# Block 0's first four SwiGLU tiles with tokens as output rows, turned back by four transposing DMAs

## The chip, the cores and the metric

The kernel runs on one core of a Trainium2 chip. The metric is the device time of one launch in microseconds (us), median of several runs of the same program. A profiled execution of the same program gives the page and the trace: which engine did what and when.

## The reference

One layer with two branches over the same layer-normalised input, for 2048 tokens of width 512:

```python
x  = A_x                                   # [1, 2048, 512]
xn = _layernorm(x, axis=-1)
# branch A: diagonal state space, 512 complex states
dt      = exp(log_dt);  Lam_bar = exp(dt * Lam)
Bu      = einsum("bld,pd->blp", xn, ((Lam_bar - 1) / Lam)[:, None] * Bmat)
h_t     = Lam_bar * h_{t-1} + Bu_t         # over the 2048 tokens
yA      = 2 * einsum("blp,dp->bld", h, Cmat).real + xn * Dskip
# branch B: SwiGLU, F = 1792
yB      = (silu(xn @ w1) * (xn @ w3)) @ w2
return x + yA + yB
```

Inputs and output are bf16.

## The kernel before

The 2048 tokens are cut into 4 blocks of 512 (`TBLK`), a block into 4 chunks of 128 tokens (`CPB`). For each block b the kernel makes these things:

- **The normalised block.** `xn_blk[b]` holds it with tokens on the partitions, `xnT_blk[b]` turned, with the width on the partitions (4 parts `dt` of 128). Block 0 is turned by TensorE in four pieces, one for each chunk (`ln_first_transpose`, L236), copied out of PSUM by ScalarE (L244). Blocks 1 to 3 are turned by transposing DMAs on SP (`ln_transpose`, L246).
- **The gates** (`glu`, L581; the last block in `glu_last`, L838). F is 14 tiles of 128 (`NFT`). For a tile f, TensorE (PE) makes gate and up, each 4 matmuls with a 128x128 piece of w1 or w3 as the stationary operand and 512 tokens of xnT streaming (L587). So the output has F on the partitions and tokens along the row. ScalarE (ACT) takes both out of PSUM as bf16, one with Silu, one as a copy (`evac`, L596 and L597), into a pair of tiles `g16`, `u16` for two f. VectorE (DVE) multiplies such a pair (`gate`, L604) into `act(b)`, a tile of 22 columns k of 128 for each chunk: 14 gates and 8 state parts. `act` has two buffers, `g16` and `u16` three each, gate and up four PSUM banks (`ps_gu`).
- **The states.** `bu` (L444), or `bu_fast` (L760) for blocks 2 and 3, makes the inputs u of the recurrence. `bu_fast` uses a product scheme with 7 instead of 8 products: sums of quarters are multiplied, and two quarters of u are a product in PSUM plus a shared product `s5` (`add`, L792, on DVE). `ssm_tasks` (L462) turns u by the angle tables `tabe` (`pre_a`, `pre_b`, `pre_c`), scans it (L505) and turns it back into `act(b)` (`post_a` to `post_c`); some of the sums there are accumulating DMAs issued from GpSimd's queue (POOL).
- **The output** (`y_fast`, L1036): gates and states of two chunks against w2 and the turned C, also with 7 products (L1054), with sums of rows by DVE (`row_sums`, L992: L1000) or by accumulating DMAs ahead of it. DVE's adds (L1065, L1139) and ACT's copies (L1077) read the products out of PSUM.

PE's order is written out by hand. DVE's order is that of a small planner, `Filler`: background tasks with costs are put out when the planned DVE time is not more than a lead past the planned PE time. Matmul groups move PE's clock (`bg.tensor(1.72)` for a tile f), and work that must stand at its place moves DVE's (`bg.own`). ACT's spare steps stand in a list of their own, `sins`: the Sin tables (L384) and other steps, of which one is taken for each f.

**The start of block 0** is special. w1 and w3 come in pieces: tiles 0 and 1 first, then 2 and 3, then the rest (`load_w`, L155). The first `FIRST` = 3 tiles are made in quarters, one for each chunk of tokens, as the chunks come ready. They have six PSUM banks (`first_ps`: four of `ps_gu`, two of `ps_bu`):

```python
637            quarter(0, (0, 1), 2)
638            quarter(1, (0, 1))
639            pps = params_transpose()
...
643            ln_first_transpose(2)
644            quarter(0, (2,))
645            ln_first_transpose(3)
646            quarter(1, (2,))
...
649            quarter(2, range(FIRST))
650            for f in range(FIRST):
651                quarter(3, (f,))
```

From f = 3 on the usual loop runs, and at f = 8 (`MID`) it puts block 0's `bu` in.

**SP's queue** at that time holds, in order: the loads of `bulk_loads`, the four transposes of block 1, then `late_loads` (L182: w2, dskip, x of blocks 2 and 3).

Of the kernel before, what the change touches and what calls it, by code (L numbers as in the profile page):

```python
# [11 lines left out]
ALU = mybir.AluOpType  # L12
# [5 lines left out]
P = 128  # L18
# [45 lines left out]
def kernel(  # L64
# [29 lines left out]
    FIRST = 3  # L94
# [87 lines left out]
    def late_loads():  # L182
        nc.sync.dma_start(out=w2_sb, in_=B_w2.rearrange("(t p) d -> p t d", p=P))
        nc.sync.dma_start(out=dskip_row, in_=A_Dskip.partition_broadcast(P))
        load_x(2, 4)
        load_x(3)

# [3 lines left out]
                for i in range(2 * FIRST)]  # L191
# [235 lines left out]

    def act_gates(b, f):
        k0, k1 = k_gate(f), k_gate(f + 1)
        return act(b)[:, :, k0:k1 + 1:k1 - k0, :].rearrange("p c k t -> p k c t")  # L430
# [31 lines left out]
    def ssm_tasks(b, posts_last=False, between=(), middle=(), late=()):  # L462
# [5 lines left out]
        def half(hf):  # L468
# [3 lines left out]
            def pre_a():  # L472
                if b == 0:
                    sin_step((2 * hf + 1, 1))
                    nc.vector.tensor_scalar(out=tabe[:, psl, 2, :], in0=tabe[:, psl, 1, :], scalar1=-1.0,
                                            scalar2=None, op0=ALU.mult)
                st["g"] = u_blk[b, hf]
                if (b, hf) == (3, 0):
                    st["p"] = up.tile(FULL, BF16, name="u")
                elif b == NBLK - 1:  # L480
                    st["p"] = xtp.tile([P, NDT, TBLK], BF16, name="xnT").rearrange("p (j r) t -> p j r t", r=2)
                else:
                    st["p"] = ssmw.tile(FULL, BF16, name="p")
                nc.vector.tensor_tensor(out=st["p"][:, :, ::-1, :], in0=st["g"], in1=tabe[:, psl, 2:0:-1, :],
                                        op=ALU.mult)

            def pre_b():
                nc.vector.tensor_tensor(out=st["g"], in0=st["g"], in1=tabe[:, psl, 0:1, :].to_broadcast(FULL),  # L488
                                        op=ALU.mult)
# [91 lines left out]
    def glu(b):  # L581
# [26 lines left out]
        if b == 0:  # L608
            f0 = FIRST
            tiles = first_ps  # L610

            def quarter(cl, fs, parts=1):
                tsl = slice(cl * P, (cl + 1) * P)
                n = NDT // parts
                for side, w in ((0, w1_sb), (1, w3_sb)):
                    for i in range(0, NDT, n):
                        for f in fs:
                            for dt in range(i, i + n):
                                nc.tensor.matmul(out=tiles[2 * f + side][:, tsl], lhsT=w[:, dt, f * P:(f + 1) * P],  # L619
                                                 rhs=xnT[:, dt, tsl], start=(dt == 0), stop=(dt == NDT - 1))  # L620

            ln_stats(0, 0)
# [14 lines left out]
            quarter(0, (0, 1), 2)  # L637
            quarter(1, (0, 1))
# [17 lines left out]
            bg.tensor(0.0)  # L656
            bg.fill()
        for f in range(f0, NFT):
# [101 lines left out]
    def bu_fast(b, hf):  # L760
# [9 lines left out]
        s5 = glup.tile([P, 2, TBLK], BF16, name="g16").bitcast(FP32).rearrange("p a t -> p (a t)")  # L770
# [19 lines left out]
        def add(out, ps):  # L790
            bg.own(0.7)
            nc.vector.tensor_tensor(out=out, in0=parts(ps), in1=parts(s5), op=ALU.add)  # L792
# [490 lines left out]
```

## Time and profile before

| | |
|---|---|
| time, 3 runs | 201.09 us median (201.04, 201.09, 201.39) |
| profiled execution, span from the first to the last instruction | 199.5 us |
| profiled execution, own time | not listed beside the three runs; their median is 1.59 us above the span |
| granted TensorE clock in the span | 0.999 of full speed |
| busy: PE matmul, DVE, ACT, POOL | 195.6, 181.8, 135.0, 51.5 us |
| DMA | 25.12 MB, mean 126 GB/s |

Busy time is the sum of an engine's instructions. PE's matmuls overlap each other in the pipeline, so their spacing in the chain is a better price for one than its own duration. PEld is TensorE's loading of the stationary operand. In a line of the trace "L619" is line 619 of the kernel, "out<-in" names the tiles, and a part in brackets says how long the engine was idle ahead of it and what ended that. "Landing" of a DMA is the time from its issue to its completion.

### The profile page before, as it was taken

To read this page: it belongs to the slowest core of one execution; us is meant where nothing else is said; L and a number is where in the kernel's file an instruction comes from. 1 tells how busy PE (TensorE), PEld (TensorE's weight loads), DVE (VectorE), ACT (ScalarE), POOL (GpSimd) and SP (SyncE) were. 2 spreads that over 40 slices of the span, in tenths; PEclk is the share of its full clock that TensorE was granted. 3 is DMA by queue.
4 is the path that set the end of the run, shared out by engine and by line. 5 is a ranking of instruction groups with operands and counts; after the bars stand their busy time and mean duration, and the time that the engine had idled before them with its cause. 6 is when DMAs were issued, how large, how long until landed. Compare 5 with 4: busy or idle time off the path is not lost.

```text
span 199.5 us, 3700 instructions
## 1 busy us (share of the span) xinstructions
PE 195.6 (98%) x1401; PEld 130.7 (65%) x1401; DVE 181.8 (91%) x254; ACT 135.0 (68%) x281; POOL 51.5 (26%) x75
## 2 busy tenths in 40 slices
PE   8999999999999999999999999999999999999994
PEld 2774444444444488866555468888566678888893
DVE  3689699999999999989999997999999999999972
ACT  4699897699999996968998684362588783111220
POOL 7180289700411134041202305040021303310000
PEclk9999999999999999999999999999999999999999
DMA  4999996991497054730997455838137732941111
GB/s 138 326 277 200 302 186 124 343 273 23 69 181 141 0 105 82 135 105 0 156 148 119 89 92 98 172 83 132 53 59 129 149 56 52 174 92 36 53 44 40
DMA packets 32258, 25.12 MB, mean 126 GB/s; under 512 B 16240, under 2 KB 29936, under 8 KB 32240
## 3 DMA queue, kind: packets, MB, share of 16 engines
q0 software_dynamic: 6128, 11.38, 33.5%
q1 hardware_dynamic: 25536, 13.21, 26.8%
q10 hardware_dynamic: 576, 0.30, 0.5%
q8 instruction: 11, 0.18, 0.4%
q14 instruction: 7, 0.06, 0.1%
HBM read 7.74 MB, written 2.10 MB: 49 GB/s over the span
## 4 chain that ended last, share of the span: by engine, by line
PE 95%; DMA 2%; SPq 1%; issue 0%; DVE 0%
PE gu_ps L587 34%; PE gu_ps L1054 17%; PE y_ps L1054 10%; PE gu_ps L848 7%; PE bu_ps L1054 7%; PE bu_ps L454 3%; PE y_ps L454 3%; PE y_ps L869 3%; PE y_ps L780 3%; DMA w_sb<-in_B_w_dram 2%; PE gu_ps L619 2%; PE gu_ps L780 2%; PE bu_ps L869 1%; PE bu_ps L780 1%; PE bu_ps L619 1%; SPq L166 0%
## 5 line engine op out<-in xcount | busy, mean ns | idle before, releaser
L587 PE MATMUL gu_ps<-xnT,w_sb 128*128 128x512 bf16 x312 | 69.6, 379 | 0.0
L587 PEld LDWEIGHTS <-w_sb 128*128 128x128 bf16 x312 | 30.5, 98 | 34.2
L1054 PEld LDWEIGHTS <-act 128*128 128x128 f16 x462 | 43.5, 98 | 5.4
L596 ACT ACTIVATE g<-gu_ps 128x512 bf16<-128x512 f32 x41 | 24.8, 606 | 6.0 <-PE gu_ps L587 3.6
L597 ACT ACTIVATE u<-gu_ps 128x512 bf16<-128x512 f32 x41 | 24.8, 606 | 4.5 <-PE gu_ps L587 3.7
L505 DVE TENSOR_TENSOR_SCAN u<-rho,ends,u 128x512 bf16<-128x512 f32 x16 | 20.0, 1270 | 0.0
L527 POOL DMA_DIRECT2D act<-p x7 | 9.2, 1320 | 34.0 <-DVE act L519 22.1
L1054 PE MATMUL gu_ps<-w_sb,act 128*128 128x256 bf16 (+3 forms) x126 | 16.0, 267 | 0.0
L848 PE MATMUL gu_ps<-xnT,w_sb 128*128 128x512 bf16 x64 | 15.9, 379 | 0.0
L604 DVE TENSOR_TENSOR act<-g,u 128x1024 f16<-128x1024 bf16 x21 | 14.2, 679 | 0.4 <-ACT u L597 0.4
L860 ACT ACTIVATE g<-gu_ps 128x512 bf16<-128x512 f32 x14 | 8.4, 599 | 5.4 <-PE gu_ps L848 5.0
L454 PEld LDWEIGHTS <-bt 128*128 128x128 bf16 x64 | 6.3, 98 | 7.5
L1077 ACT ACTIVATE x_blk<-gu_ps 128x256 f32<-128x256 f32 (+1 forms) x9 | 3.3, 368 | 10.6 <-PE gu_ps L1054 10.6
L1054 PE MATMUL bu_ps<-w_sb,act 128*128 128x256 bf16 (+3 forms) x84 | 10.4, 264 | 0.0
L1054 PE MATMUL gu_ps<-ct,act 128*128 128x256 f16 (+1 forms) x72 | 10.4, 267 | 0.0
L848 PEld LDWEIGHTS <-w_sb 128*128 128x128 bf16 x64 | 6.3, 98 | 4.8
L505 DVE TENSOR_TENSOR_SCAN u<-rho,u 128x512 bf16<-128x512 f32 x8 | 9.2, 1206 | 0.0
L1054 PEld LDWEIGHTS <-x_blk 128*128 128x128 f16 x88 | 8.6, 98 | 1.0
L1054 PEld LDWEIGHTS <-tw 128*128 128x128 f16 x88 | 8.6, 98 | 1.0
L513 DVE TENSOR_TENSOR p<-u,tabe 128x2048 f16<-128x2048 bf16 (+1 forms) x8 | 8.7, 1085 | 0.1
L519 DVE TENSOR_TENSOR act<-u,tabe 128x2048 f16<-128x2048 bf16 (+1 forms) x8 | 8.7, 1083 | 0.0
L488 DVE TENSOR_TENSOR u<-u,tabe 128x2048 bf16<-128x2048 bf16 x7 | 8.5, 1219 | 0.1
(203 smaller groups left out, 392.5 us busy)
## 6 DMA issues: line engine op xcount, KB each, us to landing
act<-p POOLq DMA_DIRECT2D x6, 512.0 KB, 6.1
xn<-x_blk POOLq DMA_DIRECT2D x4, 512.0 KB, 5.5
out_dram<-xn SPq DMA_DIRECT2D x15, 128.0 KB, 1.7
w_sb<-in_B_w_dram SPq DMA_DIRECT2D x1, 1792.0 KB, 8.2
act<-act POOLq DMA_DIRECT2D x5, 352.0 KB, 4.6
w_sb<-in_B_w_dram SPq DMA_DIRECT2D x2, 768.0 KB, 6.4
u<-p POOLq DMA_DIRECT2D x3, 512.0 KB, 5.1
w_sb<-in_B_w_dram SPq DMA_DIRECT2D x4, 256.0 KB, 4.9
```

What stands on the lines that cost most here:

```text
L454: nc.tensor.matmul(out=ps, lhsT=bt[:, ri, dt, pt * P:(pt + 1) * P], rhs=xnT_blk[b][:, dt, :], start=(dt == 0), stop=(dt == NDT - 1))
L505: nc.vector.tensor_tensor_scan(out=v, data0=rho[:, pt:pt + 1].to_broadcast([P, TBLK]), data1=v, initial=init, op0=ALU.mult, op1=ALU.add)
L513: nc.vector.tensor_tensor(out=by_state(st["p16"][:, csl]), in0=by_chunk(st["g"][:, :, ::-1, tsl]), in1=by_chunk(tabe[:, psl, 2:0:-1, tsl]) ...
L519: nc.vector.tensor_tensor(out=by_state(act_state(b, hf)[:, csl]), in0=by_chunk(st["g"][:, :, :, tsl]), in1=by_chunk(tabe[:, psl, 0:1, tsl] ...
L527: gp.dma_start(out=a, in_=p16, accum_op=ALU.add)
L587: nc.tensor.matmul(out=ps[:, tsl], lhsT=w[:, dt, f * P:(f + 1) * P], rhs=xnT[:, dt, tsl], start=(dt == 0), stop=(dt == NDT - 1))
L596: nc.scalar.activation(out=g16[:, f % 2, :], in_=g_ps, func=ACT.Silu)
L597: nc.scalar.activation(out=u16[:, f % 2, :], in_=u_ps, func=ACT.Copy)
L604: nc.vector.tensor_tensor(out=act_gates(b, f - 1), in0=split(g16), in1=split(u16), op=ALU.mult)
L780: nc.tensor.matmul(out=out[:, h * TH:(h + 1) * TH], lhsT=left[:, h, k, :], rhs=right[:, k, :], start=(start and h == 0 and k == 0), stop=( ...
L848: nc.tensor.matmul(out=ps, lhsT=w[:, dt, f * P:(f + 1) * P], rhs=xnT[:, dt, :], start=(dt == 0), stop=(dt == NDT - 1))
L1054: nc.tensor.matmul(out=out, lhsT=left[:, k, :], rhs=right[k][:, cols], start=(start and k == 0), stop=(k == NK - 1), skip_group_check=True)
```

## The change

The first four tiles of block 0 (`FIRST` = 4) are made the other way round. The chunk of xnT is the stationary operand and the columns of w1 or w3 stream, so the output has 128 tokens on the partitions and columns of F along the row: for the chunks 0 and 1 in two halves of 256 columns (A and B, as the weights come), for the chunks 2 and 3 in 512 columns at once. Each chunk has a bank for gate and one for up; those of chunk 3 come from `ps_y`. ACT takes out a chunk's gate and up (`evac_rows`), DVE multiplies two chunks at a time (`gate_rows`) into a part of `act(1)` that is not in use yet (`first_products`), and four transposing DMAs at the end of `late_loads` turn the products back into `act(0)`, one for each chunk.

The diff also changes the state inputs of block 3: where DVE added a product in PSUM and `s5`, ACT now copies the product to u in fp16, and an accumulating DMA from POOL's queue adds `s5`, now fp16 too. `pre_a` and `pre_b` read that u as fp16 and write bf16 in its place.

```diff
-    FIRST = 3
+    FIRST = 4
...
         load_x(2, 4)
         load_x(3)
+        for c in range(CPB):
+            nc.sync.dma_start_transpose(out=act(0)[:, c, 0:FIRST, :], in_=first_products()[:, c, :])
...
+    def first_products():
+        return act(1)[:, :, 2 * NK - FIRST:2 * NK, :].rearrange("p c k t -> p c (k t)")
...
-                st["g"] = u_blk[b, hf]
+                st["v"] = u_blk[b, hf]
+                st["g"] = st["v"].bitcast(BF16) if b in (3,) else st["v"]
...
-                nc.vector.tensor_tensor(out=st["p"][:, :, ::-1, :], in0=st["g"], in1=tabe[:, psl, 2:0:-1, :],
+                nc.vector.tensor_tensor(out=st["p"][:, :, ::-1, :], in0=st["v"], in1=tabe[:, psl, 2:0:-1, :],
...
-                nc.vector.tensor_tensor(out=st["g"], in0=st["g"], in1=tabe[:, psl, 0:1, :].to_broadcast(FULL),
+                nc.vector.tensor_tensor(out=st["g"], in0=st["v"], in1=tabe[:, psl, 0:1, :].to_broadcast(FULL),
...
-            tiles = first_ps
-
-            def quarter(cl, fs, parts=1):
-                tsl = slice(cl * P, (cl + 1) * P)
+            act(0)
+            tiles = [first_ps[2 * c:2 * c + 2] for c in range(CPB - 1)]
+
+            def rows(cl, side, fsl, parts=1):
                 n = NDT // parts
-                for side, w in ((0, w1_sb), (1, w3_sb)):
-                    for i in range(0, NDT, n):
-                        for f in fs:
-                            for dt in range(i, i + n):
-                                nc.tensor.matmul(out=tiles[2 * f + side][:, tsl], lhsT=w[:, dt, f * P:(f + 1) * P],
-                                                 rhs=xnT[:, dt, tsl], start=(dt == 0), stop=(dt == NDT - 1))
-
+                w = (w1_sb, w3_sb)[side]
+                for i in range(0, NDT, n):
+                    for dt in range(i, i + n):
+                        nc.tensor.matmul(out=tiles[cl][side][:, fsl], lhsT=xnT[:, dt, cl * P:(cl + 1) * P],
+                                         rhs=w[:, dt, fsl], start=(dt == 0), stop=(dt == NDT - 1))
+
+            def evac_rows(cl):
+                if cl % 2 == 0:
+                    pair[:] = [glup.tile([P, 2, TBLK], BF16, name="g16"), glup.tile([P, 2, TBLK], BF16, name="u16")]
+                nc.scalar.activation(out=pair[0][:, cl % 2, :], in_=tiles[cl][0], func=ACT.Silu)
+                nc.scalar.activation(out=pair[1][:, cl % 2, :], in_=tiles[cl][1], func=ACT.Copy)
+
+            def gate_rows(cl, g16, u16):
+                bg.own(0.6, -0.5)
+                nc.vector.tensor_tensor(out=first_products()[:, cl:cl + 2, :], in0=g16, in1=u16, op=ALU.mult)
+
+            A, B, AB = slice(0, 2 * P), slice(2 * P, 4 * P), slice(0, 4 * P)
...
-            quarter(0, (0, 1), 2)
-            quarter(1, (0, 1))
+            for side in range(2):
+                for cl in range(2):
+                    rows(cl, side, A)
             pps = params_transpose()
...
             ln_first_transpose(2)
-            quarter(0, (2,))
+            for cl in range(2):
+                rows(cl, 0, B)
             ln_first_transpose(3)
-            quarter(1, (2,))
+            for cl in range(2):
+                rows(cl, 1, B)
...
-            quarter(2, range(FIRST))
-            for f in range(FIRST):
-                quarter(3, (f,))
-            evac(0, tiles[0], tiles[1])
-            evac(1, tiles[2], tiles[3])
-            evac(2, tiles[4], tiles[5])
-            gate()
+            for side in range(2):
+                rows(2, side, AB)
+            tiles.append([ps_y.tile([P, TBLK], FP32, name="y_ps") for _ in range(2)])
+            for side in range(2):
+                rows(3, side, AB)
+            evac_rows(0)
+            evac_rows(1)
+            gate_rows(0, *pair)
+            evac_rows(2)
+            evac_rows(3)
+            late = list(pair)
...
+            if b == 0 and f == FIRST:
+                gate_rows(2, *late)
...
-        s5 = glup.tile([P, 2, TBLK], BF16, name="g16").bitcast(FP32).rearrange("p a t -> p (a t)")
+        by_dma = b in (3,)
+        if by_dma:
+            u = u.bitcast(FP16)
+            s5 = glup.tile([P, 2, TBLK], BF16, name="g16").bitcast(FP16)[:, 0, :]
+        else:
+            s5 = glup.tile([P, 2, TBLK], BF16, name="g16").bitcast(FP32).rearrange("p a t -> p (a t)")
...
         def add(out, ps):
+            if by_dma:
+                copy(out, parts(ps))
+                gp.dma_start(out=out, in_=parts(s5), accum_op=ALU.add)
+                return
             bg.own(0.7)
             nc.vector.tensor_tensor(out=out, in0=parts(ps), in1=parts(s5), op=ALU.add)
```

More of the change, by code (lines that the diff above doesn't have):

```diff
@@ L186, in late_loads @@
         load_x(3)
+        for c in range(CPB):
+            nc.sync.dma_start_transpose(out=act(0)[:, c, 0:FIRST, :], in_=first_products()[:, c, :])
     ones = nc.const_aps.tensor(1.0, (P, TBLK), BF16)
     first_ps = [(ps_gu if i < 4 else ps_bu).tile([P, TBLK], FP32, name="gu_ps" if i < 4 else "bu_ps")
-                for i in range(2 * FIRST)]
+                for i in range(6)]
     wps = first_ps[-1]
```

## The prediction

> **What bounds the kernel now.** I read the page first: engine shares, then the chain that ended last.
>
> ```profile
> PE 195.6 (98%) x1401; PEld 130.7 (65%) x1401; DVE 181.8 (91%) x254; ACT 135.0 (68%) x281; POOL 51.5 (26%) x75
> ...
> PE 95%; DMA 2%; SPq 1%; issue 0%; DVE 0%
> ```
>
> TensorE (PE) is the chain for 95% of the span. VectorE (DVE) at 91% is nearly as full, but nothing on the chain waits for it. Next the chain in order of time (start, length, what), which shows where PE work begins to follow PE work:
>
> ```profile
> 2.58 4.53 DMA w_sb<-in_B_w_dram
> 7.11 0.05 issue
> 7.16 1.51 PE gu_ps L619 x24
> 8.67 0.11 PE y_ps L315
> 8.78 0.33 PE y_ps L243 x4
> 9.11 0.58 PE bu_ps L619 x8
> 9.69 0.22 PE y_ps L243 x4
> 9.92 0.45 PE bu_ps L619 x8
> ...
> 13.04 8.63 PE gu_ps L587 x40
> ...
> 196.16 0.63 PE gu_ps L1054 x11
> ```
>
> The first w3 piece lands at 7.11 (issued 2.58). From there to 196.79 every piece is PE with no idle piece between, so a microsecond off PE's work or its start is a microsecond off the end, as long as nothing else becomes late; and nothing taken from DVE, ACT or POOL can shorten this chain by itself. Paces: 8 matmuls of 128 columns take 0.45 (55.8 ns each), 40 of 512 columns 8.63 (215.7 ns), 11 of 256 columns 1.20 (109.2 ns). The x8 at 9.11 takes 0.13 more than 0.45: the second w3 piece, issued 3.69, lands near 9.3 (its landing taken from the issue view: two issues with median 5.4, one of them 5.2, so 5.6).
>
> Last the timeline of the start (start, length, engine, line, [idle before <- releaser]):
>
> ```profile
> 6.27 0.62 PE L619 MATMUL gu_ps<-xnT,w_sb 128*128 128x128 bf16 x8
> 6.29 0.60 ACT L244 ACTIVATE xnT<-y_ps 128x512 bf16<-128x512 bf16 x1 [0.23 <-PE y_ps L243]
> ...
> 7.16 1.51 PE L619 MATMUL gu_ps<-xnT,w_sb 128*128 128x128 bf16 x24 [0.27 <-DMA w_sb<-in_B_w_dram]
> ```
>
> PE has only chunk 0's w1 half (8 matmuls, 0.45) to do before w3 is there: it is done at 6.72 and stands 0.44 until 7.16. Chunk 1 of xnT is ready at 6.89.
>
> **The change, part by part.** *PE's front.* Removed: 96 matmuls of 128 columns (96 x 55.8 ns = 5.36) and tile 3's 8 of 512 (1.73): 7.08. Added: 32 of 256 columns (32 x 109.2 ns = 3.49) and 16 of 512 (3.45): 6.95. Work: -0.14. Order: now both chunks' w1 halves come before w3. Chunk 0 runs 6.27 to 6.71, chunk 1 starts when its copy is out, 6.89 plus some 0.06 = 6.95, and w3, landed at 7.11, is asked for only at 7.39. The stand falls from 0.44 to 0.24: -0.20. The second w3 piece is now asked for after the transposes of chunk 3, near 10, behind 9.3: -0.13. Sum -0.47: PE would start tile 4 at 14.30 instead of 13.04 + 1.73 = 14.77. I keep the 0.28 that the chain shows around L315 and the transposes after it (1.51 against 24 x 55.8 ns = 1.34, and 0.33 against 0.22); were those gone too, the sum would be -0.75.
>
> *ACT's front.* 8 evacuations before (L596, L597 for tiles 0 to 3), 8 after, same shape; ACT starts them at 11.96, after its table load, and is through at 15.80 in both. PE asks for tile 4's buffers at 14.30 (free at about 12.6), tile 6's at 17.75 (tile 4's copy, now ahead of the three Sin steps, out at about 16.4), tile 7's at 19.5 (free at about 18.1): margins over 1 us, so 0 on the path. bt lands at 13.54 + 5.0 = 18.5 and is read from 21.2. w1 and w3 for tiles 4 to 7 land by 12.3.
>
> *Gates.* Two products of 128x1024 by DVE before (L604, 0.66 to 0.69) and two after. Then four transposing DMAs on SP, behind the last x load (SP is through with it at 36.54 and then waits 40.4 us for the next block's norm). The nearest row is the same transfer of another tile, xnT<-xn: 1.2 to 2.8 us of SP each, 2.4 to 7.0 to landing, so 42 to 49 for the last one. The first reader is DVE's row sum at L1000, 59.50. Cover 10 us or more: 0. If it were gone, DVE's whole queue would wait behind that sum.
>
> *The planner.* Tile 3 no longer adds 1.72 to its clock, so DVE's background work is put out one tile later against gates and adds; the Sin of table (1,1) moves behind block 0's fourth state copy and ends near 26.0, where DVE took it at 25.52. DVE is then some 0.4 later until about 78, while PE is 0.47 earlier: 0.9 of margin is used. The tightest consumer I find is the sum s4 of the first output pair: DVE ends it at 74.65, PE reads it at 76.03, margin 1.38, left 0.5. From 78 to 87 DVE waits for PE three times (0.36, 0.48, 0.57), so it is in step again. Taken: 0; without this margin up to 0.5.
>
> *Block 3's state inputs.* DVE loses four adds (L792, 0.67 each, 2.7 in all). ACT gains four copies (nearest row L785, 0.60): they fall into its idle times of 1.0 to 2.4 between 120 and 141. POOL gains four accumulating DMAs of 128 KB (0.85 to 1.3 of its queue each); the queue sat idle 8.85 before 132.16 and 11.7 before 146.06, and the DMA queued behind them (act<-tw, L1093) comes at 132.16. Landing: 1.7 (128 KB plain store) to 4.3 (256 KB accumulate), I take 4, the nearer kind: at 142 at the latest, read by DVE at 146.7 and 151.2. On PE's path 0. DVE's freed time lets scans move ahead:
>
> ```profile
> 132.88 2.45 DVE L505 TENSOR_TENSOR_SCAN u<-rho,ends,u 128x512 bf16<-128x512 f32 x2
> ...
> 135.25 0.67 DVE L792 TENSOR_TENSOR x_blk<-gu_ps,g 128x512 bf16<-128x512 f32 x1
> ...
> 135.83 0.41 DVE L1065 TENSOR_TENSOR q<-y_ps,xn 128x256 f32<-128x256 f32 x1
> ...
> 137.48 1.36 PE L1054 MATMUL y_ps<-tw 128*128 128x256 f16 x11
> ```
>
> PE writes y_ps again at 137.48 only when the L1065 add has read it (136.24): margin 1.24. After the change three scans (3 x 1.27) stand there where two scans and an add stood, 0.6 more: margin 0.6.
>
> All in all -0.47. The profiled span is 199.5, and its own time is listed only by the runs: the median 201.09 lies 1.59 above the span, which I keep. 199.5 - 0.47 + 1.59 = 200.6. About 0.2% (0.4 us) is what a measurement of this kernel can tell from no change, so the forecast stands just outside.
>
> **The rivals.** *A, the gain is taken back:* PE comes 0.47 earlier to something that has its own time (a copy by ACT, DVE's s4 at margin 0.5, the add at margin 0.6) and stands there up to that long: 200.7 to 201.1. For: DVE has no gap from 14 to 59. Against: every margin I could follow stays positive.
>
> *B, slower, DVE's order:* the background scans put in front of an add that frees PE's PSUM. Place: L1065 before product 7 of the output pairs in 117 to 140. If the planner's order, or a scan that waits for its accumulating DMA, makes DVE one scan (1.27) later there than I follow, PE stands 1.27 - 0.6 = 0.7 at one pair and as much again at the next: -0.47 + 1.3 = +0.9, 202.0. It decides from 0.6 of DVE lateness on. For: 91% DVE, and its order there is new. Against: DVE has 2.7 less to do just there.
>
> *C, weight loads on the path:* 104 weight loads become 48. If narrow matmuls were paced by their loads (98 ns each in the rows of L619), 56 x 98 ns = 5.5 would go: 195.6. Against: 8 matmuls of 128 columns pass in 0.45, so the loads overlap. The Trainium skill ("TensorE: Matmul & The Clock Gate", section "Back-to-back issue gap") gives for a sustained stream of load and matmul about 81 ns at 128 columns and 131 ns at 512; worked out from that, an estimate, with 98 at 256, the front would fall from 8.8 to 5.2, a gain of 3.6. This trace has 55.8 and 215.7 ns for the same two, and the measurement decides.
>
> That the change does not do what it says (transposes that come late) would cost first at 59.5; it is left at 1 in 100, within the rest below.
>
> **How the numbers follow.** The forecast 0.58, of which 0.07 for a gain that stays short of 0.4; A 0.15; B 0.20; C 0.02; other slowdowns 0.05. Faster 0.58 - 0.07 + 0.02 = 0.53, same 0.07 + 0.15 = 0.22, slower 0.25. The range reaches from 200.2 (the sum -0.75, and 0.15 for a run's spread) to 202.0 (B); C and the other slowdowns are left out. The forecast's own range is 200.3 to 200.9.
>
> **What would show it.** Right: two w1 groups of 256 columns before the first w3 one, an idle of about 0.24 at 6.7, tile 4 starting near 14.3, and no stand of PE after that; the four transposes on SP between 36 and 42; DVE lower by some 2.7. Wrong: an idle piece between PE pieces of the chain with DVE or ACT as its releaser (A, B, by its place), or tile 4 starting before 13 (C).

## The result, and the profile after

The kernel with the change takes 201.57 us (median of 22 runs, 201.11 to 203.44) against 201.13 for the kernel before (22 runs, 200.67 to 201.70): ratio 1.0036, 95% interval 1.0020 to 1.0052. It is slower by 0.2% in the median and by about 0.4% in the ratio, which counts the long runs more. The forecast was 200.6, faster; the measured median lies inside the range.

The runs after the change fall in two groups: 14 from 201.11 to 201.98 with a median of 201.29, and 8 from 202.46 to 203.44. The kernel before has no run above 201.70. The profiled execution after the change took 202.56 and is of the upper group. So two things have to be explained: why the lower group is not 0.5 below the kernel before, and what the upper group is.

The page, the engines' totals and the chain's shares by engine:

```profile
PE 194.5 (97%) x1332; PEld 129.0 (64%) x1345; DVE 179.8 (90%) x250; ACT 137.3 (68%) x285; POOL 56.3 (28%) x79
...
PE 86%; DMA 5%; ACT 4%; issue 1%; POOL 1%; SPq 1%; DVE 0%; POOLq 0%
```

PE has 1.1 us less to do and DVE 2.0, ACT 2.3 more and POOL 4.8. But PE is no longer the chain from the first weights to the end: 86% instead of 95%, and DMA, ACT and POOL have come in. The chain in order of time (start, length, what) shows the front, and then the place where it leaves PE:

```profile
2.13 4.06 DMA w_sb<-in_B_w_dram
...
6.23 0.60 PE gu_ps L624 x4
...
6.86 1.48 PE gu_ps L624 x12
...
14.20 6.91 PE gu_ps L593 x32
...
81.00 6.50 DMA xnT<-xn
87.50 0.14 issue
87.64 0.38 PE gu_ps L593
```

Tile 4 starts at 14.20; before it was 14.77. This lead of 0.57 is kept up to 86.26. There PE asks for block 2's first tile and stands 1.4, until the last of the four transposing DMAs that turn block 2's `xn` has landed at 87.50. Before, that DMA was issued at 82.82 and landed at 85.22, and PE came to it at 86.83 (L587) without a stand:

```profile
xnT<-xn SPq DMA_TRANSPOSE x1, 2.4
```

(A landing here and below is the issue plus the view's time to landing, good to 0.05.) Behind 87.64 nothing more is lost on PE. Counted from matmul start to matmul start the stand costs 1.54. With the front's -0.57 and the 0.27 by which the end of the program is longer (shown below) that makes 1.24; the two spans differ by 1.23.

What the profile of before had no trace of at all stands much earlier, on DVE. The timeline of DVE after the change, at the second half of block 0's states:

```profile
47.25 1.22 DVE L511 TENSOR_TENSOR_SCAN u<-rho,u 128x512 bf16<-128x512 f32 x1
49.47 1.23 DVE L519 TENSOR_TENSOR p<-u,tabe 128x2048 f16<-128x2048 bf16 x1 [1.00 <-DMA act<-p]
```

DVE stands 1.00 before L519 (`post_a`). It wants to write a buffer `p`, and the accumulating DMA `act<-p` of the first half, issued from POOL at 38.49, still reads it. The view of DMA issues, 34 to 50 us, after the change (KB each, median us to landing):

```profile
x_blk<-in_A_x_dram SPq DMA_DIRECT2D x1, 512.0 KB, 8.9
act<-p POOLq DMA_DIRECT2D x1, 512.0 KB, 10.9
...
act<-act SPq DMA_TRANSPOSE x4, 8.8
```

and its line for the same transfer before:

```profile
act<-p POOLq DMA_DIRECT2D x1, 512.0 KB, 9.1
```

Before, it was issued at 37.56 and landed at 46.6; DVE came to `post_a` (there L513) at 47.69 and did not wait:

```profile
45.34 2.31 DVE L505 TENSOR_TENSOR_SCAN u<-rho,u 128x512 bf16<-128x512 f32 x2
47.69 1.22 DVE L513 TENSOR_TENSOR p<-u,tabe 128x2048 f16<-128x2048 bf16 x1
```

After, it lands at 49.4, and DVE has come for the buffer at 48.47. The four new transposing DMAs `act<-act` are in flight in just that stretch.

### The profile page after: what moved, and what is told of

It is laid out like the page before. It is cut to its first block, busy times and chain, and to the rows that moved or that the text cites. A ratio compares the mean times of both kernels' runs of the same rounds, so it can differ in the third digit from the quotient of the medians.

```text
span 200.8 us, 3594 instructions
## 1 busy us (share of the span) xinstructions
PE 194.5 (97%) x1332; PEld 129.0 (64%) x1345; DVE 179.8 (90%) x250; ACT 137.3 (68%) x285; POOL 56.3 (28%) x79
## 4 chain that ended last, share of the span: by engine, by line
PE 86%; DMA 5%; ACT 4%; issue 1%; POOL 1%; SPq 1%; DVE 0%; POOLq 0%
PE gu_ps L593 33%; PE gu_ps L1088 13%; PE y_ps L1088 7%; PE gu_ps L882 7%; PE bu_ps L1088 5%; PE y_ps L459 3%; PE bu_ps L459 3%; PE y_ps L903 3%; PE y_ps L810 3%; DMA xnT<-xn 3%; DMA w_sb<-in_B_w_dram 2%; PE gu_ps L624 2%; PE gu_ps L810 2%; PE bu_ps L903 1%; PE bu_ps L810 1%
## 5 line engine op out<-in xcount | busy, mean ns | idle before, releaser
L593 PE MATMUL gu_ps<-xnT,w_sb 128*128 128x512 bf16 x297 | 67.2, 379 | 1.7 <-DMA xnT<-xn 1.4
L593 PEld LDWEIGHTS <-w_sb 128*128 128x128 bf16 x304 | 29.7, 98 | 35.1 <-issue 1.6
L602 ACT ACTIVATE g<-gu_ps 128x512 bf16<-128x512 f32 x38 | 22.9, 602 | 6.3 <-PE gu_ps L593 5.2
L603 ACT ACTIVATE u<-gu_ps 128x512 bf16<-128x512 f32 x38 | 23.0, 604 | 4.7 <-PE gu_ps L593 4.3
L882 PE MATMUL gu_ps<-xnT,w_sb 128*128 128x512 bf16 x61 | 15.6, 379 | 0.1
L610 DVE TENSOR_TENSOR act<-g,u 128x1024 f16<-128x1024 bf16 x19 | 12.9, 679 | 0.0
L894 ACT ACTIVATE g<-gu_ps 128x512 bf16<-128x512 f32 x14 | 8.4, 599 | 5.4 <-PE gu_ps L882 4.5
L1088 PE MATMUL bu_ps<-w_sb,act 128*128 128x256 bf16 (+3 forms) x84 | 10.4, 264 | 0.0
L1088 PE MATMUL gu_ps<-ct,act 128*128 128x256 f16 (+1 forms) x72 | 10.4, 267 | 0.0
L519 DVE TENSOR_TENSOR p<-u,tabe 128x2048 f16<-128x2048 bf16 (+1 forms) x8 | 8.7, 1088 | 1.1 <-DMA act<-p 1.0
L882 PEld LDWEIGHTS <-w_sb 128*128 128x128 bf16 x64 | 6.3, 98 | 4.8
L1041 POOL DMA_DIRECT2D act<-act x5 | 4.9, 976 | 13.8 <-DVE tw L1034 11.0
```

What stands on the lines that cost most here:

```text
L519: nc.vector.tensor_tensor(out=by_state(st["p16"][:, csl]), in0=by_chunk(st["g"][:, :, ::-1, tsl]), in1=by_chunk(tabe[:, psl, 2:0:-1, tsl]) ...
L593: nc.tensor.matmul(out=ps[:, tsl], lhsT=w[:, dt, f * P:(f + 1) * P], rhs=xnT[:, dt, tsl], start=(dt == 0), stop=(dt == NDT - 1))
L602: nc.scalar.activation(out=g16[:, f % 2, :], in_=g_ps, func=ACT.Silu)
L603: nc.scalar.activation(out=u16[:, f % 2, :], in_=u_ps, func=ACT.Copy)
L610: nc.vector.tensor_tensor(out=act_gates(b, f - 1), in0=split(g16), in1=split(u16), op=ALU.mult)
L882: nc.tensor.matmul(out=ps, lhsT=w[:, dt, f * P:(f + 1) * P], rhs=xnT[:, dt, :], start=(dt == 0), stop=(dt == NDT - 1))
```

## The experiments

Time is the median; "before" in a row is the kernel before, run beside it on the same chip. The ratio is that of all runs, not of the medians. A stand is given as the views have it, the idle time of the engine.

**Parts of the change.** The first idea was that the planner's clock, which lacks tile 3, puts `u<-p` (the accumulating DMA of block 1's second half, `pre_c`) beside block 2's transposes: in the profile after the change it is issued at 79.66 instead of 76.40, and the last two of the four transposes take 5.9 and 6.5 to land instead of 2.5 and 2.4.

*The front alone*, block 3 as before:

```diff
-        by_dma = b in (3,)
+        by_dma = b in ()
...
-                st["g"] = st["v"].bitcast(BF16) if b in (3,) else st["v"]
+                st["g"] = st["v"]
```

> The change without its block 3 part (DVE adds s5 there as before). Theory T (the planner's clock lacks tile 3, so pre_b of block 1's second half and its accumulating DMA u<-p are put out later, at 79.7 instead of 76.4 us, beside the transposes that turn block 2, and PE waits for xnT near 87): same time as the change, 201.3 to 202.3, PE idle 0.5 to 2 near 87. Rival U (the four added transposes slow later DMAs): the same as T here. Rival V (block 3's copies and DMAs cost the time): 200.6, no idle near 87.

Measured: 202.47 (6 runs) against 201.09, ratio 1.0071 (1.0052 to 1.0089). The front alone is slower than the whole change. Its profile has the same two stands (DVE 1.62 before L519; PE 0.3 at block 2's xnT), and a new one of 0.5 near 191, where PE waits for the `act` sums of DVE. So DVE is late at the end without block 3's relief.

*Block 3's state inputs alone*, on the kernel before:

```diff
...
+        by_dma = b in (3,)
+        if by_dma:
+            u = u.bitcast(FP16)
+            s5 = glup.tile([P, 2, TBLK], BF16, name="g16").bitcast(FP16)[:, 0, :]
...
         def add(out, ps):
+            if by_dma:
+                copy(out, parts(ps))
+                gp.dma_start(out=out, in_=parts(s5), accum_op=ALU.add)
+                return
```

> The kernel before with the block 3 part alone. T and U: no cost on PE's path, 201.0 to 201.2, DVE lower by 2.7 us, PE without idle after its start. V: 201.6 to 202.

Measured: 201.81 (10 runs) against 201.09, ratio 1.0036 (1.0022 to 1.0050). Its chain:

```profile
131.91 0.50 POOL act L528
...
132.65 6.65 DMA act<-tw
...
139.34 1.37 PE bu_ps L1064 x11
```

The relieved DVE finishes `post_b` earlier, so on POOL `act<-p` (L528) goes ahead of `act<-tw`. That DMA then takes 6.65 to land, and PE waits 0.5 for it. In the whole change `act<-tw` stands ahead (133.13, then `act<-p` at 133.89), lands in 3.9, and nobody waits.

*The whole change with tile 3's 1.72 given back to the planner's clock:*

```diff
             bg.tensor(0.0)
             bg.fill()
+            sin_step((0, 0))
+            bg.tensor(1.72)
+            bg.fill()
...
-            if b == 0 and f == FIRST:
-                sin_step((0, 0))
-            elif b > 0 or f != MID - 1:
+            if b > 0 or f != MID - 1:
                 sin_step()
```

> The whole change, with tile 3's 1.72 us put back on the planner's clock (and the Sin step (0,0) taken where it was), so that DVE's order up to block 3 is that of before. T: u<-p is issued near 76 again, xnT lands before 86.3, no idle of PE near 87, and the front's gain arrives: 200.5 to 200.7. U: the idle near 87 stays, 201.3 to 202.3. V: 201.6 or more, with an idle of PE after 117.

Measured: 203.18 (6 runs) against 201.09, ratio 1.0098 (1.0080 to 1.0116). The first idea fell: `u<-p` is issued at 76.83, near the 76.40 of before, and PE still waits 0.6 for xnT (its last two transposes are issued at 81.18 and 82.49 and land after 5.1 and 4.3) and 0.5 for `act<-tw`, behind `act<-p` as in the run above. The profiled execution, 202.45, is the fastest of the six, so what makes the others 0.7 slower is not in it and stays open.

*The clock alone*, on the kernel before:

```diff
-            bg.tensor(1.72)
+            if b > 0 or f > FIRST:
+                bg.tensor(1.72)
```

> The kernel before, its rows and gates as they were, with tile 3's 1.72 us taken off the planner's clock and nothing else. T: u<-p is issued near 79.7, block 2's xnT lands 0.3 to 1.5 us after PE wants it at 86.8, 201.4 to 202.5. U and V: no change, 201.0 to 201.2.

Measured: 202.27 (6 runs) against 201.09, ratio 1.0057 (1.0040 to 1.0074). The view of PE's waits:

```profile
PE y_ps L1055 <- DVE act L525: 0.5, 1, 0.5
```

So the planner's shift by one tile is not free. By itself it makes DVE late near 191 (the view has 0.5, but PE's matmuls from 162.75 to its last one take 1.03 longer than the same ones before), and it puts `u<-p` at 79.09, so that the last xnT transpose lands at 86.38, where PE comes for it and loses 0.3. In the whole change block 3's relief of DVE removes the first of these, and the second stays.

**Block 2's xnT.** Four kernels on one chip, before 201.09 (35 runs).

*No `u<-p` beside the transposes:* block 1's second `pre_c` becomes a DVE add.

```diff
-                if b == 0 or (b, hf) == (2, 0):
+                if b == 0 or (b, hf) in ((1, 1), (2, 0)):
...
```

> The whole change, with one transfer less: the second half of block 1's state input is summed by one DVE add instead of the accumulating 512 KB DMA u<-p of line L501, which in the changed kernel was issued at 79.66 and ran beside the last two of block 2's four transposing DMAs (they landed 5.9 and 6.5 us after their issue; before, with no such DMA beside them, 2.5 and 2.4). Theory N (the cost is block 2's xnT, held up by that DMA): all four transposes land 2.4 to 3.5 us after issue, the last by about 84, PE's wait of 1.4 at 87 is gone, PE starts block 2 at 86.3, the span is 199.3 to 199.7 and the median 200.7 to 201.0, unless the DVE add (1.1 us more on an engine busy for 90%) brings a new wait. Theory R (the 1.4 is only where slack shows, and later waits hold the end anyway): xnT comes earlier, but the time stays at 201.5 with a new wait near 139 or 191. Theory P (the late landing is from something else, the power of POOL or the transposes themselves): landings stay at 4 to 6.5 us and the wait at 87 stays.

Measured: 201.21 (11 runs), ratio 1.0009 (0.9998 to 1.0021). The landings are 2.4 to 3.2, the last at 84.21, and no PE wait: the accumulating DMA is what slows the transposes. But the time is 201.2, not 200.7 to 201.0. One run of the eleven, 202.19, is above 201.7. In this profile DVE stands 1.44 before L519, and its execution (201.40) is of the lower group all the same.

*The squares one step earlier:*

```diff
-    ln_scalar_engine(2, lambda cl: xn_blk[2][:, cl, :], sins, (0, 1, 4))
+    ln_scalar_engine(2, lambda cl: xn_blk[2][:, cl, :], sins, (0, 0, 5))
```

> The whole change, with ACT's four squares of block 2 put one step earlier (pauses 0, 0, 5 instead of 0, 1, 4): the orders on DVE, POOL and SP are those of the changed kernel, on ACT one square moves ahead of one tile's evictions and the last one ahead of one copy. Theory N: the squares end about 0.6 earlier (72.9 instead of 73.5), so POOL's power and the norm start about 0.6 earlier (75.6) and the four transposes too; half of them are out of the way when u<-p is issued, PE's wait at 87 goes from 1.4 to at most 0.8 and the median from 201.6 to 200.9 to 201.2. Theory R: the wait at 87 shrinks but the time does not. Theory P: the wait at 87 stays at 1.4.

Measured: 201.21 (12 runs, two of them 202.44 and 202.53), ratio 1.0015 (0.9999 to 1.0032). The last landing is 85.67 and PE does not wait in the profile, though DVE stands 1.11 before L519.

*Plain copies instead of turning ones:*

```diff
-            nc.sync.dma_start_transpose(out=act(0)[:, c, 0:FIRST, :], in_=first_products()[:, c, :])
+            nc.sync.dma_start(out=act(0)[:, c, 0:FIRST, :], in_=act(1)[:, c, 2 * NK - FIRST:2 * NK, :])
```

> The whole change, but the four new DMAs copy the products straight into act(0) instead of turning them, so the first four gates of block 0 keep tokens where features should be; all orders are those of the changed kernel. Theory U (DMA transposes from the front leave their mark on later transposes): block 2's transposes land in 2.4 to 3.5 us, the wait at 87 goes, 200.7. Theory N: nothing changes: the wait at 87 is 0.5 to 1.5 and the median 201.4 to 201.8.

Measured: 201.22 (12 runs, one of them 202.43), ratio 1.0013 (1.0000 to 1.0027). Neither theory: the last two transposes of block 2 still land after 6.2 and 5.3, but PE does not wait; and in this profile `act<-p` lands in 9.2 and DVE does not stand before L519.

*The kernel before with the same move, (0, 0, 5):*

> The kernel before with the same move of block 2's squares, as the control for the run with that move in the changed kernel: before, block 2's last transpose landed at 85.2 and PE came to it at 86.83, so by theory N xnT has 1.6 to spare and an earlier one is worth nothing: 200.9 to 201.3, the same as before. By theory P, or if the kernel before too sometimes waits there, it gains 0.2 to 0.5.

Measured: 201.06 (12 runs), ratio 0.9999 (0.9989 to 1.0009), as expected.

All three cures left the time at 201.2 with no PE wait in the profile, and spans of 199.4 to 199.6. PE's last matmul ended 0.2 to 0.4 earlier than before, and yet the spans were level. That led to the end of the program.

**The end of the program.** From the last DVE add to the end of the span, before:

```profile
core 0 of [0], span 199.5 us
...
196.81 0.29 DVE L1065 TENSOR_TENSOR xn<-gu_ps,q 128x128 bf16<-128x128 f32 x1 [0.27 <-PE gu_ps L1054]
```

and after the change:

```profile
core 0 of [0], span 200.8 us
...
197.78 0.29 DVE L1099 TENSOR_TENSOR xn<-gu_ps,q 128x128 bf16<-128x128 f32 x1 [0.27 <-PE gu_ps L1088]
```

2.7 has become 3.0, with the same add, the same store behind it and the same landing. The trace's records of SP's closing waits, counted from that add (us):

```
before  0.42 0.49 0.55 0.62 0.68 0.74 1.30 1.51 1.82   first drain 1.89
after   0.41 0.48 1.30 1.53 1.85 1.91 1.97 2.03 2.09   first drain 2.16
```

SP ends with one wait for each of eight semaphores of hardware transfers, in fixed order, and the transfers take the eight in turn. Before, the last three stores hold numbers 5, 6 and 7, so all other waits are passed while the stores fly. With four transfers more they hold 1, 2 and 3, and after the last landing four more waits follow (not five, as the expectation below has it), 60 ns each, before the drain. With 0.02 by which the wait for that landing itself is later, the drain comes 0.27 later. The waits are read from the trace's records of SP: the eight are passed in the same order in both kernels, and each kernel's hardware transfers (56 and 60) take the eight in turn.

Four more transfers among the late loads, the same bytes, undo this in the changed kernel and cause it in the kernel before:

```diff
-        nc.sync.dma_start(out=dskip_row, in_=A_Dskip.partition_broadcast(P))
+        for i in range(2):
+            dsl = slice(i * D // 2, (i + 1) * D // 2)
+            nc.sync.dma_start(out=dskip_row[:, dsl], in_=A_Dskip[dsl].partition_broadcast(P))
         load_x(2, 4)
-        load_x(3)
+        load_x(3, 4)
```

*In the changed kernel:*

> The whole change, and four transfers more among the late loads (block 3 of x in four parts instead of one, the Dskip row in two halves: the same bytes). With the four transposing DMAs that makes eight more transfers on the hardware queues than in the kernel before. Theory L (the end of the program): SP closes the kernel with one wait for each of eight transfer semaphores in a fixed order, 60 ns each, and the transfers take the eight in turn. Before, the last three stores hold numbers 5, 6 and 7, the last ones waited for; with four transfers more they hold 1, 2 and 3, and five waits, 0.27 us, stand behind the last landing (from the last DVE add to the end of the span 2.72 before against 2.98 after). With eight more they hold 5, 6 and 7 again: that stretch is 2.7 and the fastest runs are 0.27 below those of the changed kernel, 200.85; the wait of block 2 for xnT is left as it is and still lengthens some runs to over 202. Rival: the stretch is 2.95 again (it belongs to the four added transposes or to the front), and the time that of the changed kernel, 201.2 to 201.6.

Measured: 200.88 (11 runs, 200.74 to 201.27) against 200.83 (35 runs), ratio 1.0003 (0.9994 to 1.0012).

```profile
core 0 of [0], span 199.0 us
...
196.33 0.29 DVE L1101 TENSOR_TENSOR xn<-gu_ps,q 128x128 bf16<-128x128 f32 x1 [0.27 <-PE gu_ps L1090]
```

The stretch is 2.7 again. No run is above 201.27 either, which was not expected: in this profile the four turning DMAs, now behind the parts of x, are issued from 41.10 on, land in 3.3 (median), and `act<-p` lands in 8.7. With the end cured and no upper group, the front's gain of some 0.2 should now show, but the ratio allows at most 0.12 of it. The four loads may cost the rest, as the next run suggests.

*In the kernel before:*

> The kernel before with the same four transfers more among the late loads and nothing else. Theory L: the last stores hold semaphores 1, 2 and 3, the stretch from the last DVE add to the end is 2.95 instead of 2.70 and the time 0.2 to 0.3 longer, 201.3 to 201.4 (ratio 1.001 to 1.0015). Rival: the stretch stays at 2.7 and the time at 201.1.

Measured: 201.25 (12 runs) against 200.83, ratio 1.0028 (1.0015 to 1.0040).

```profile
core 0 of [0], span 199.9 us
...
196.90 0.29 DVE L1067 TENSOR_TENSOR xn<-gu_ps,q 128x128 bf16<-128x128 f32 x1 [0.27 <-PE gu_ps L1056]
```

The stretch is 3.0. Of the 0.42 it explains 0.27; where the other 0.15 comes from is not shown.

*Both cures (early squares, four loads):*

> The whole change with both cures: block 2's squares one step earlier on ACT, so that xnT comes in time more often, and the four more transfers among the late loads, so that the last stores hold the last semaphores. By the theory N and L together: front gain 0.3 kept (PE reaches block 2 at 86.3 without a wait), end stretch 2.7: span 199.1 to 199.2, median 200.8 to 200.95, ratio 0.9985 to 0.9993 against the kernel before: faster than both. If one of the two is wrong: 201.1 to 201.3.

Measured: 201.07 (12 runs) against 200.83, ratio 1.0009 (0.9994 to 1.0025). The stretch is 2.7, but the time is not below the kernel before: no version here is shown to beat it.

*The control:*

> The changed kernel as it is, as the control on the same chip for the others of this group: median 201.3 to 201.7, with a third or more of its runs between 202.4 and 203.5.

Measured: 201.25 (12 runs, two of them 202.59 and 202.65), ratio 1.0033 (1.0015 to 1.0050). On this chip the upper group is a sixth of the runs, not a third.

**The front by itself.** Two kernels that end behind block 1's last gate were to time it. The cut of the kernel before also has the four more loads.

```diff
     gate = glu(1)
     gate()
-    bg.flush(("sums", 0))
...
+    k = k_gate(NFT - 2)
+    nc.sync.dma_start(out=ov[:, CPB, 0:2 * P].bitcast(FP16),
+                      in_=act(1)[:, 0, k:k + 2, :].rearrange("p k t -> p (k t)"))
```

> The kernel before (with the four more loads, so that it holds as many hardware transfers as the other cut), ended behind block 1's last gate: blocks 0 and 1 without their output products and nothing of blocks 2 and 3; one store of the last gates closes it. Its time is that of PE's first 69.9 us and a fixed end, 73 to 76 us; the wait for xnT, the end phase and block 3 are not in it, and both cuts close on the same semaphore (number 2 of eight). What matters is the difference to the other cut, in the same rounds. Theory K (the front's gain is real in every run, 0.3 to 0.5 as the profiles show, and lost later): the cut of the changed kernel is 0.3 to 0.5 shorter. Theory J (the profiled executions flatter the change, since the wait for the second weights that it removes is long only there): the two are within 0.15.

> The changed kernel, ended at the same place (behind block 1's last gate, one store). Theory K: 0.3 to 0.5 below the cut of the kernel before. Theory J: within 0.15 of it, though the profiles of the two still differ by 0.3 or more.

Measured: 79.03 (4 runs, before) and 81.95 (6 runs, after). Neither theory, because DVE, not PE, ends these kernels. PE is through at 69.96 and 69.66. DVE ends 2.5 later in the cut of the changed kernel (its last product starts at 75.55 instead of 73.03), and the store behind it takes 1.1 longer to land. DVE's timeline says why it is late:

```profile
51.88 1.23 DVE L519 TENSOR_TENSOR p<-u,tabe 128x2048 f16<-128x2048 bf16 x1 [3.21 <-DMA act<-p]
```

What this measured by accident is the stand of DVE before L519, three times as long as in the first profile. The cut of the kernel before has none.

**Later squares**, in the changed kernel and in the kernel before:

```diff
-    ln_scalar_engine(2, lambda cl: xn_blk[2][:, cl, :], sins, (0, 1, 4))
+    ln_scalar_engine(2, lambda cl: xn_blk[2][:, cl, :], sins, (0, 2, 3))
```

> The changed kernel with block 2's squares one step later on ACT (pauses 0, 2, 3 instead of 0, 1, 4), the opposite of the earlier run. Theory N (in the changed kernel block 2's xnT has little or nothing to spare): the squares and with them the four transposing DMAs come 0.6 to 1.7 later, PE waits for xnT in nearly every run, 0.5 to 2, and the median is 201.8 to 203. If xnT had room: no wait, 201.2.

Measured: 202.91 (6 runs) against 201.11, ratio 1.0083 (1.0059 to 1.0106). As a test of xnT it says little, since DVE stands here too:

```profile
51.98 1.23 DVE L519 TENSOR_TENSOR p<-u,tabe 128x2048 f16<-128x2048 bf16 x1 [3.16 <-DMA act<-p]
```

DVE's order is that of the changed kernel, and all of it behind L519 is 2.7 later than in the control's profile. At 75.9 PE comes for the sum s4 of the first output pair and stands 1.4; `u<-p` is issued at 82.16 and the last xnT transpose lands at 88.19.

> The kernel before with the same move. Theory N: its last transpose landed 1.6 before PE came to it, so a delay of 0.6 is taken up whole and one of 1.7 just about: 200.8 to 201.3 as before. If before too has no room: 201.5 or more.

Measured: 201.44 (12 runs) against 201.11, ratio 1.0013 (1.0001 to 1.0026): a little slower if at all, no PE wait in the profile, the last landing at 85.78.

**The stand before L519.** Across the profiles of the kernel before and its variants DVE never stands there; in those of the changed kernel and its variants it stands 0.35 to 3.2 unless `act<-p` lands within about 9. The wait was taken away by another tile, no order changed:

```diff
...
-                    st["p16"] = ssmw.tile(FULL, BF16, name="p").bitcast(FP16)...
+                    if (b, hf) == (0, 1):
+                        home = xn_blk[2].rearrange("p (j r) t -> p j r t", r=2)
+                    else:
+                        home = ssmw.tile(FULL, BF16, name="p")
+                    st["p16"] = home.bitcast(FP16)...
...
```

> The whole change, all orders as in it; only the products that DVE's L519 writes for block 0's second half of states go into a tile that is still free (xn of block 2) instead of into the buffer p that the accumulating DMA act<-p of the first half is still reading. Theory D (the upper runs come from there): in the changed kernel the four transposing DMAs stand beside that 512 KB DMA, it lands 10.4 to 13.1 after its issue instead of 7.7 to 10.1, DVE stands 0.5 to 3.2 before L519 at 48.5, and everything that DVE does later, block 1's and 2's sums of states and the first output pair's s4 among it, comes that much later. With another tile DVE goes on at 48.5 whatever the landing: no idle of DVE before L519, DVE's s4 of the first pair at 73 or earlier, no run above 201.9, median 201.1 to 201.3 (the end of the program still costs its 0.27). If the upper runs come from block 2's xnT by itself, they stay: some runs at 202.4 to 203.5, as in the changed kernel.

Measured: 201.14 (11 runs, 201.05 to 201.42) against 201.06, ratio 1.0007 (0.9999 to 1.0016). DVE's timeline, and the DMA issue that it no longer waits for:

```profile
47.61 1.22 DVE L512 TENSOR_TENSOR_SCAN u<-rho,u 128x512 bf16<-128x512 f32 x1
48.86 1.23 DVE L524 TENSOR_TENSOR xn<-u,tabe 128x2048 f16<-128x2048 bf16 x1
```

```profile
act<-p POOLq DMA_DIRECT2D x1, 512.0 KB, 13.7
```

`act<-p` lands later here than in any other profile, 13.7 after its issue, and it costs nothing: DVE goes on at once, and none of the eleven runs is of the upper group. On this chip `act<-p` lands after 13.1 and 13.0 in the cut and in the later squares, which have the same orders up to there, and DVE stands 3.2 in both. So by these runs the upper group needs that wait. It is not the wait alone: without `u<-p` beside the transposes, or with these earlier, a stand of 1.4 or 1.1 was followed by no stand of PE. The changed kernel as it is was not run beside this one. If its upper group came as rarely as in the control, 2 of 12, eleven runs without one would still come up by chance once in seven times, and once in 140 at the 8 of 22 of the result.

The four turning DMAs ahead of the late loads:

```diff
     def late_loads():
+        for c in range(CPB):
+            nc.sync.dma_start_transpose(out=act(0)[:, c, 0:FIRST, :], in_=first_products()[:, c, :])
         nc.sync.dma_start(out=w2_sb, in_=B_w2.rearrange("(t p) d -> p t d", p=P))
...
         load_x(3)
-        for c in range(CPB):
-            nc.sync.dma_start_transpose(out=act(0)[:, c, 0:FIRST, :], in_=first_products()[:, c, :])
```

> The whole change with the four transposing DMAs ahead of the late loads on SP instead of behind them; the orders of all other engines as in it. They are issued at about 30.5 instead of 35 to 37 and land before act<-p is issued at 38.6; the loads of w2, Dskip and x come 5 to 8 later and have room. Theory D: act<-p lands 8 to 10 after its issue as in the kernel before, DVE does not stand before L519, no upper runs: 201.1 to 201.3, like the run above. If it is the loads and not the transposing DMAs that hold act<-p up, its landing stays at 10.4 to 13 and DVE's idle with it.

Measured: 202.20 (6 runs, 201.83 to 202.77) against 201.06, ratio 1.0054 (1.0037 to 1.0071). The expectation was wrong. The issues between 28 and 50:

```profile
act<-p POOLq DMA_DIRECT2D x1, 512.0 KB, 11.9
...
act<-act SPq DMA_TRANSPOSE x4, 2.5
```

The turning DMAs land in 2.5 now, but the loads of w2 and x now come later (w2 is issued at 37.17 instead of 30.57) and run beside `act<-p`, which lands in 11.9, and DVE stands 2.05. So the turning is not needed for a late landing: the loads beside `act<-p` do it as well. That the turning has no part is not shown. On one chip, plain copies of the same bytes left `act<-p` at 9.2, where two profiles with turning copies have 11.0 and 11.3.

## Why the prediction was wrong, point by point

**The step that failed most: the gates' four DMAs.** The prediction gave them "Cover 10 us or more: 0", because their first reader comes at 59.5. That reader never waited. But the step looked only at who reads the new transfers, not at which transfers are in flight beside them. `act<-p` had about 1.0 to spare before (landed 46.6, wanted at 47.69), and with 512 KB more in flight it came up to 3.2 late. Without this wait the upper group, 8 of 22 runs, is not seen. How the stand becomes time: DVE's work behind it comes later, and with it `u<-p` and the last xnT transpose, or, with a stand of 2 and more, s4 of the first output pair. Against the kernel with its own tile for L519, a stand of 1.0 moves `u<-p` by 0.3, one of 2.05 by 2.0, one of 3.16 by 2.8.

| profile | DVE stands before L519 | `u<-p` issued | last xnT landing | PE asks | PE stands at xnT or s4 |
|---|---|---|---|---|---|
| before | 0 | 76.40 | 85.22 | 86.8 | 0 |
| own tile for L519 | 0 | 79.38 | 85.92 | 86.6 | 0 |
| control | 0.51 | 79.44 | 86.19 | 86.6 | 0 |
| changed kernel | 1.00 | 79.66 | 87.50 | 86.3 | 1.4 |
| early squares | 1.11 | 79.94 | 85.67 | 86.5 | 0 |
| no `u<-p` there | 1.44 | none | 84.21 | 86.6 | 0 |
| front alone | 1.62 | 80.59 | 86.83 | 86.7 | 0.3 |
| turning DMAs first | 2.05 | 81.38 | 87.42 | 87.5 | 0.3 |
| later squares | 3.16 | 82.16 | 88.19 | 88.2 | 1.4 |

In the last two the stand at s4 comes first, so that PE reaches xnT later. The landing also varies by itself: the last transpose of the changed kernel took 6.5 and that of the control 5.4, which is more of the difference between the two than the 0.2 by which it was issued later. What made that one slow is not shown. With 0.4 of margin left some runs wait and some don't.

**The planner: "Taken: 0; without this margin up to 0.5".** Mis-sized. The clock alone cost the kernel before 1.2 (ratio 1.0057), at two places of which the prediction had neither. In the whole change, without the stand before L519, it costs nothing by itself (the sum for the lower group, below, leaves nothing for it), but it takes the margin. The prediction followed DVE's readers of the first output pair, with margins that were right (s4 in the changed kernel: DVE done at 74.7, wanted at 75.5), and did not follow what DVE's order releases on the DMA queues. `u<-p` moved from 76.40 to 79.4 without any stand, beside block 2's transposes, and the margin of xnT fell from 1.6 to about 0.5. xnT was not on its list of consumers at all.

**PE's front: -0.47.** Right in kind, too large. The work fell as counted, the order is as described, and the first profile shows even -0.57 (14.20 against 14.77). But one pair of profiles is not the mean. PE reaches block 0's `bu` at 21.44 on average over seven profiles with the old front (21.04 to 21.60) and at 21.23 over thirteen with the new one (20.95 to 21.62): -0.21, an estimate, since each set is spread over more than 0.5.

Which terms were mis-sized shows when the front is divided at the place where the wait ends, the first w3 matmul of the old front and the first matmul of chunk 1 in the new one. From there to `bu` the old front takes 14.22 in six of its seven profiles, the new one 14.09 in all thirteen: the -0.14 of work is right (0.13). The -0.13 for the second w3 piece was a stand that only the profile of before has (14.36). The place itself moves from 7.20 to 7.15 on average, -0.05 where the prediction has -0.20. Both stands, counted as the prediction does, were longer than its own figures: before w3 0.61 on average instead of 0.44, before chunk 1 0.42 in eleven of the thirteen profiles instead of 0.24. So they fall by the 0.2 of the forecast. But the prediction let both fronts start at 6.27, and on average the first gate matmul starts at 6.32 in the new one and at 6.14 in the old one, which takes nearly all of it back. Why the new one starts later is not shown.

The own time of the execution that the prediction leaned on was some 201.3 to 201.4, at least 0.2 above the median: in the other profiles own time and span differ by 1.77 to 1.87, where the prediction had put 1.59 between them.

**What was not in the sum: the end, +0.27.** The stretch is shown both ways by the four loads. In the control's profile the front and the end are all there is: PE reaches `bu` 0.28 earlier, stands nowhere behind it, the end is 0.27 longer, and the span is that of before, 199.5. On average over the profiles -0.21 + 0.27 = +0.06, and with L519's wait taken away the changed kernel measures +0.08 (201.14 against 201.06; the ratio allows -0.02 to +0.32).

**Block 3's state inputs: 0 on the path.** Right in the whole change. DVE's adds are gone, the four copies and DMAs delay nobody, the landings are 5.3 and 6.4 (medians of two each) where 4 was taken, and the L1065 add (now L1099) is done at 137.8 with PE there at 138.44: the margin of 0.6 is there. Alone it costs 0.7, through the order on POOL.

**The rivals.** A foresaw that the gain would be taken back by something with its own time, and this is what happened in the lower group, though by the end of the program and not by a copy or add. B had the right engine for the upper group, DVE, but too small a size (202.0, where the group's median is 202.9) and the wrong place: not an add in 117 to 140, but a buffer at 48. C did not occur.

## What to carry to other kernels

A new transfer is priced by its neighbours, not only by its reader: list the transfers in flight in the same stretch, above all accumulating ones whose source is a buffer that will be written again, with their margins. A gain of a few tenths at the front should be taken from several profiles, since the wait that it removes can vary by as much. And where the count of transfers changes, look at the end of the program too: the last stores may move in the order of the closing waits.

## What the runs showed of the hardware that was not expected

- A 512 KB accumulating DMA lands 4.5 after its issue with little else in flight (`u<-p` of block 1's first half), and 7.7 to 13.7 with loads and transposes beside it (`act<-p`). The other way round, a transposing DMA of block 2 lands in 2.4 to 2.5 alone (once 3.2) and in 2.9 to 6.5 beside `u<-p`. That the two kinds delay each other agrees with the Trainium skill ("DMA: Bandwidth & Descriptors", section "Queues, rings and completion order"): each DMA engine goes round between the queues that have work for it, a packet at a time.
- The closing waits of SP take 60 ns each once their transfers are done, so that the position of the last stores among the eight semaphores is worth up to 0.27 here.
- POOL's power on 128x4 (the rstd of block 2) took 1.04, 1.36 or 1.64 in different profiles of kernels with the same code for it. What decides it was not tried.

What stays open: the spread of `act<-p`'s landing from run to run and chip to chip (10.4 to 13.7 in profiles with the changed kernel's orders), how much of it is the turning, why the last transpose of block 2 took 6.5 in the upper group's one profile of the changed kernel, and the 0.15 that the four more loads cost the kernel before.
